# Linear attention with an MLP behind it: q of batches 1 to 7 transposed by a DMA instead of TensorE, input weights loaded in 64-partition pieces

## The chip, the cores and the metric

One core of a Trainium2 chip runs the whole kernel. The metric is device time in microseconds (us); the kernel before took 325.62 us, the median of three runs between 323.76 and 325.9.

## The reference

The shapes are batch 8, 8 heads, 576 positions, head dimension 64; the MLP goes from 512 to 2048 and back.

```python
def _attn_ref(q, k, v):
    q_s = np.exp(q - np.max(q, axis=-1, keepdims=True))
    q_s = q_s / (np.sum(q_s, axis=-1, keepdims=True) + 1e-09)
    k_s = np.exp(k - np.max(k, axis=2, keepdims=True))
    k_s = k_s / (np.sum(k_s, axis=2, keepdims=True) + 1e-09)
    kv = np.einsum('bhsd,bhse->bhde', k_s, v)
    return np.einsum('bhsd,bhde->bhse', q_s, kv)

def _moe_ref(x, w_in, w_out):
    h = x @ w_in
    g = h * (1.0 / (1.0 + np.exp(-h)))
    return g @ w_out

x = attn_out.transpose(0, 2, 1, 3).reshape(B * S, H * D)
```

The heads of a position, 8 times 64 values, stand side by side as the 512 columns of x, of which there are 8 times 576, or 4608 rows.

## The kernel before, in words

**Attention of one batch.** `load` brings q, k and v of a batch, 1152 KB each, from SP's queue into tiles of 128 partitions (two heads by 64 position groups; a partition holds 9 positions, J). `exp` takes exp on ACT to bf16 (`eq`, `ek`). `qsum` and `qnorm` normalise q: sums and reciprocals on DVE, the product on DVE or POOL. `vcast` turns v to bf16 in `vaug`, with a column of ones beside each head, so that `kv` on TensorE (PE), over 9 values of j, gives the products of k and v and the sums of k at once. `kvcopy` on DVE divides them and puts them as blocks into `kvbd`. `tr` transposes the normalised q: three groups of six 128x128 transposes on PE into PSUM (`qtps`), each copied to `qT` by `trcopy` on DVE (lines 116 to 137). `xt` multiplies `kvbd` with `qT`, the projection, once for each of four chunks of 128 columns of x, and copies the result out of PSUM to `XT`, on ACT from tile 1 on.

**The MLP.** The rows of x are cut into nine tiles: tile 0 is the 576 of batch 0 in two parts, tile 1 is 448, the others 512. `mm1` is one unit for each of 16 blocks of 128 of the 2048 columns: four matmuls for each part, then tanh on ACT and a product on DVE, into `GT`. `mm2` has 16 units a tile too, of four matmuls; after the last of a block of rows the result goes over `ost` (four buffers) to DRAM, as two stores on SP's queue. All weights are loaded once, at the start, by POOL's queue, which turns them from f32 to bf16: W_in (`W1`, in the trace `W_58`) in eight transfers of 256 KB, W_out (`W2`, `W_59`) in four.

**The order.** Batch 0 is written out first. Then a list `units` has mm1 of tile 0, mm2 of tile 0, mm1 of tile 1, mm2 of tile 1, and from there mm2 of one tile interleaved with mm1 of the next. `plan_attn` puts each step of a batch's attention ahead of a unit, counted from the first mm1 unit of the batch's tile: `sm` for the two halves of exp of q and of k, `tp` for the transposes, `ks` for kv, `ox` for the projections. Each engine executes what it was given in this order. SP's queue has no units of its own: a load or store there waits only for its data, its buffer and what stands ahead of it. Loads of batch 1 are held back by a one-element copy on POOL (line 399) that reads the last element of W_in. Projections and transposes share one PSUM buffer (tag `aps`).

## Time and profile before

| | |
|---|---|
| median of three runs | 325.62 us |
| the profiled execution | 325.91 us |
| its span, first to last instruction | 324.1 us |
| mean granted clock of TensorE in the span | 0.969 |
| TensorE busy | 293.5 us (91%) |
| DVE, ACT, POOL busy | 164.3, 162.3, 42.7 us |
| moved by DMA | 42.26 MB |

The span is shorter than the profiled execution by 1.8 us, which lie around it. Busy time of TensorE includes matmuls that overlap the next, so a stage with busy time near its length is full, not necessarily at its peak. A line of the timeline gives start, length, engine and line of code, instruction, the tile written and the tiles read, and in brackets the idle time ahead of it and what ended that. A granted clock of 1.0 is 2.4 GHz, 0.5 is 1.2 GHz.

### The profile page before, as it was taken

The page shows a single profiled execution, that of the slowest core. Times are in us where ns is not written, and L with a number is a line of the kernel's source. Part 1 is how long each engine was busy: PE and PEld are TensorE (multiplying, and loading weights), DVE is VectorE, ACT ScalarE, POOL GpSimd, SP SyncE. Part 2 cuts the span into 40 slices and gives each one's busy share as a digit, 9 for nine tenths or more (in the row PEclk, how much of TensorE's full clock was granted, in tenths as well). Part 3 has the DMA queues.
Part 4 walks back from the last instruction along what each step waited for, and adds up shares of the span by engine and source line. Part 5 has one row for each costly group of instructions (what it writes and reads, how often), then busy time and mean ns, then how long its engine had stood idle before and what let it go on. Part 6 is the DMA issues. An engine that isn't in the chain of part 4 may idle for free.

```text
span 324.1 us, 4484 instructions
## 1 busy us (share of the span) xinstructions
PE 293.5 (91%) x1723; PEld 142.5 (44%) x1723; DVE 164.3 (51%) x312; ACT 162.3 (50%) x266; POOL 42.7 (13%) x40
## 2 busy tenths in 40 slices
PE   5617998997889789899999999999999999999993
PEld 1404654553445334445444444444444444444441
DVE  4813889378927655753375348534543333343300
ACT  5603773278157467566465646654345446444220
POOL 0803000000007025250025003400000000000000
PEclk9976999999799989999999999999999999999998
DMA  7899999971857715758211111111201211111222
GB/s 285 181 165 144 263 329 397 392 244 20 307 183 230 271 40 209 260 172 258 74 32 34 32 32 34 32 33 34 47 22 46 49 34 32 32 32 35 64 66 66
DMA packets 28933, 42.26 MB, mean 130 GB/s; under 512 B 8944, under 2 KB 10992, under 8 KB 28912
## 3 DMA queue, kind: packets, MB, share of 16 engines
q1 hardware_dynamic: 18480, 37.76, 36.8%
q0 software_dynamic: 10432, 4.22, 9.3%
q8 instruction: 13, 0.21, 0.3%
q14 instruction: 8, 0.07, 0.1%
HBM read 36.70 MB, written 9.44 MB: 142 GB/s over the span
## 4 chain that ended last, share of the span: by engine, by line
PE 71%; DMA 10%; DVE 10%; ACT 4%; issue 2%; POOL 1%; SPq 0%; DVEq 0%; ACTq 0%
PE hps L195 35%; PE ops L228 28%; DMA W_58<-in_moe_w_in_dram 5%; DMA vt<-in_v_dram 4%; DVE zq L103 3%; DVE GT L211 2%; PE kvps L144 2%; PE ops L324 2%; ACT sg L203 2%; PE qtps L121 2%; DVE eq L109 2%; DMA kt<-in_k_dram 2%; ACT eq L89 1%; POOL W_58 L273 1%; DVE rzq L104 1%
## 5 line engine op out<-in xcount | busy, mean ns | idle before, releaser
L211 DVE SCALAR_TENSOR_TENSOR GT<-sg,hps 128x512 bf16<-128x512 f32 (+2 forms) x176 | 101.7, 587 | 126.2 <-ACT sg L203 123.2
L195 PE MATMUL hps<-XT,W_58 128*128 128x512 bf16 (+2 forms) x640 | 149.0, 364 | 9.0 <-DMA W_58<-in_moe_w_in_dram 8.9
L203 ACT ACTIVATE sg<-hps 128x512 f32<-128x512 f32 (+2 forms) x160 | 88.4, 554 | 110.5 <-PE hps L195 109.3
L228 PE MATMUL ops<-W_59,GT 128*128 128x512 bf16 x512 | 130.1, 383 | 0.0
L195 PEld LDWEIGHTS <-W_58 128*128 128x128 bf16 x640 | 61.8, 99 | 74.2 <-DMA W_58<-in_moe_w_in_dram 10.7
L228 PEld LDWEIGHTS <-GT 128*128 128x128 bf16 x512 | 49.0, 99 | 55.4 <-issue 2.0
L109 POOL TENSOR_TENSOR eq<-eq,rzq 128x1152 bf16<-128x1152 bf16 x10 | 21.1, 2117 | 143.2 <-PE hps L195 126.9
L243 ACT ACTIVATE ost<-ops 128x512 f32<-128x512 f32 x34 | 20.2, 597 | 21.7 <-PE ops L228 21.4
L103 DVE TENSOR_REDUCE zq<-eq 128x18 f32<-128x1152 bf16 x16 | 21.5, 1346 | 3.4 <-ACT eq L89 3.4
L121 PE MATMUL qtps<-ident,eq 128*128 128x128 bf16 x144 | 13.0, 233 | 8.0 <-DVE eq L109 5.4
L89 ACT ACTIVATE eq<-qt 128x1152 bf16<-128x1152 f32 x16 | 18.4, 1159 | 2.5 <-DMA qt<-in_q_dram 2.5
L89 ACT ACTIVATE ek<-kt 128x1152 bf16<-128x1152 f32 x16 | 18.3, 1160 | 1.1 <-DMA kt<-in_k_dram 1.1
L121 PEld LDWEIGHTS <-eq 128*128 128x128 bf16 x144 | 10.3, 104 | 15.6 <-DVE eq L109 6.8
L324 PE MATMUL ops<-W_59,GT 128*128 128x512 bf16 x64 | 15.3, 379 | 0.0
L136 DVE COPY qT<-qtps 128x768 bf16<-128x768 bf16 (+1 forms) x32 | 13.7, 447 | 2.4 <-PE qtps L121 2.3
L144 PEld LDWEIGHTS <-ek 64*128 64x128 bf16 x288 | 9.1, 98 | 10.6 <-issue 8.5
L324 PEld LDWEIGHTS <-GT 128*128 128x128 bf16 x64 | 6.1, 98 | 6.3
L109 DVE TENSOR_TENSOR eq<-eq,rzq 128x1152 bf16<-128x1152 bf16 x6 | 8.1, 1357 | 0.2
L144 PE MATMUL kvps<-vaug_61,ek 64*128 64x130 bf16 x144 | 5.9, 227 | 2.2 <-DVE kvbd_62 L158 2.2
L144 PE MATMUL kvps<-vaug_60,ek 64*128 64x130 bf16 x144 | 6.0, 228 | 1.8 <-ACT vaug_60 L94 1.4
L96 POOL CAST vaug_61<-vt 128x1152 bf16<-128x1152 f32 x6 | 6.8, 1156 | 0.0
L273 POOL DMA_DIRECT2D W_58<-in_moe_w_in_dram x8 | 6.5, 862 | 0.0
(138 smaller groups left out, 87.6 us busy)
## 6 DMA issues: line engine op xcount, KB each, us to landing
out_dram<-ost SPq DMA_DIRECT2D x72, 128.0 KB, 2.4
qt<-in_q_dram SPq DMA_DIRECT2D x7, 1152.0 KB, 6.5
kt<-in_k_dram SPq DMA_DIRECT2D x7, 1152.0 KB, 6.9
vt<-in_v_dram SPq DMA_DIRECT2D x7, 1152.0 KB, 6.3
W_58<-in_moe_w_in_dram POOLq DMA_DIRECT2D x8, 256.0 KB, 15.2
W_59<-in_moe_w_out_dram POOLq DMA_DIRECT2D x4, 512.0 KB, 16.1
qt<-in_q_dram SPq DMA_DIRECT2D x2, 576.0 KB, 4.1
kt<-in_k_dram SPq DMA_DIRECT2D x2, 576.0 KB, 7.1
```

Of the source, the lines that this page charges most:

```text
L89: nc.scalar.activation(out=o, in_=jgd(st[b][src], cc), func=ACT.Exp)
L103: nc.vector.reduce_sum(out=st[b]["zq"][:, cc], in_=e, axis=AX.X)
L109: eng.tensor_tensor(out=e, in0=e, in1=r[:, :, :, None].to_broadcast([128, J, 2, D]), op=ALU.mult)
L121: nc.tensor.transpose(out=t[:, i * 128:(i + 1) * 128], in_=st[b]["eq"][:, j, cc * 128:(cc + 1) * 128], identity=ident,)
L136: nc.vector.tensor_copy(o, t[:, :, i:i + n, :])
L144: nc.tensor.matmul(out=st[b]["kvps"][:, r, cc * 256:cc * 256 + 2 * E1], lhsT=st[b]["ek"][r * P:(r + 1) * P, j, cc * 128:(cc + 1) * 128], r ...
L195: nc.tensor.matmul(out=hps[:, 0:size], lhsT=W1[:, c, fb * 128:(fb + 1) * 128], rhs=XT[t][:, c, off:off + size], start=(c == 0), stop=(c == ...
L203: nc.scalar.activation(out=sg[:, 0:size], in_=hps[:, 0:size], func=ACT.Tanh, scale=0.5)
L211: nc.vector.scalar_tensor_tensor(out=GT[g][:, fb, col:col + n], in0=sg[:, h], scalar=1.0, in1=hps[:, h], op0=ALU.add, op1=ALU.mult,)
L228: nc.tensor.matmul(out=OP[t, tb], lhsT=GT[t][:, fc, tb * 128:(tb + 1) * 128], rhs=W2[:, fc, :], start=(fc == 0), stop=(fc == NFB - 1),)
L243: nc.scalar.activation(out=ost, in_=OP[t, tb], func=ACT.Copy, scale=0.5)
L324: nc.tensor.matmul(out=OP[t, tb], lhsT=GT[t][:, fc, tb * 128:(tb + 1) * 128], rhs=W2[:, fc, :], start=(fc == 0), stop=(fc == NFB - 1),)
```

## The change

The transposes of q of batches 1 to 7 leave TensorE: `tr_dma` issues one transposing DMA on SP's queue for a batch, from `eq` to `qT` in SBUF, 576 KB, in 18 blocks of 128x128; batch 0 keeps `tr` and `trcopy`. `qT` is now laid out in j blocks, so `xt` reads columns in pieces of 64. Tile 0 is cut at 320 instead of 288 columns, a multiple of 64. W_in comes in 16 transfers of 64 partitions and a quarter of the columns (the four of one quarter first), instead of eight of 128 partitions and half of the columns. Loads of batch b + 2 are planned right behind the transpose of batch b. The plans move: batch 2 is prepared from 21 units ahead instead of 11, with POOL instead of DVE for `qnorm` and `vcast`; batches 3 and 4 by a few units; the projections of batch 2 by two.

```diff
--- before.py
+++ after.py
@@ -40,7 +40,7 @@
     NCH = NT // TCH
 
     cut = [0, S] + [TCH * (t + 2) for t in range(NCH - 1)]
-    part = [[(0, S // 2), (S // 2, S // 2)]] + [[(0, cut[t + 1] - cut[t])] for t in range(1, NCH)]
+    part = [[(0, 5 * P), (5 * P, S - 5 * P)]] + [[(0, cut[t + 1] - cut[t])] for t in range(1, NCH)]
     E1 = D + 1
     assert J * P == S and D == 64 and NG == 4 and DM == H * D and NT == NCH * TCH
 
@@ -111,29 +111,34 @@
         )
 
 
+    def qt_tile(b):
+        if "qT" not in st[b]:
+            st[b]["qT"] = ap.tile([128, J, 2, 128], BF16, name="qT")
+        return st[b]["qT"]
+
+    def tr_dma(b, eng):
+        eng.dma_start_transpose(
+            out=qt_tile(b).rearrange("x j c y -> x (j c) y"),
+            in_=st[b]["eq"].rearrange("x j y -> x (j y)"),
+        )
+
     TG = 6
 
-    def tr(b, g, tag="aps"):
-        t = ps.tile([128, TG * 128], BF16, name="qtps", tag=tag, bufs=PSB[tag])
+    def tr(b, g):
+        t = ps.tile([128, TG, 128], BF16, name="qtps", tag="hps", bufs=PSB["hps"])
         st[b]["qtps", g] = t
         for i in range(TG):
             cc, j = divmod(g * TG + i, J)
             nc.tensor.transpose(
-                out=t[:, i * 128:(i + 1) * 128],
-                in_=st[b]["eq"][:, j, cc * 128:(cc + 1) * 128],
-                identity=ident,
+                out=t[:, i, :], in_=st[b]["eq"][:, j, cc * 128:(cc + 1) * 128], identity=ident
             )
 
     def trcopy(b, g):
-        if "qT" not in st[b]:
-            st[b]["qT"] = ap.tile([128, 2, 2, J * P], BF16, name="qT")
-        t = st[b]["qtps", g].rearrange("x (j r p) -> x r j p", r=2, p=P)
         i = 0
         while i < TG:
             cc, j = divmod(g * TG + i, J)
             n = min(J - j, TG - i)
-            o = st[b]["qT"][:, cc, :, j * P:(j + n) * P].rearrange("x r (j p) -> x r j p", p=P)
-            nc.vector.tensor_copy(o, t[:, :, i:i + n, :])
+            nc.vector.tensor_copy(qt_tile(b)[:, j:j + n, cc, :], st[b]["qtps", g][:, i:i + n, :])
             i += n
 
     def kv(b, cc):
@@ -177,7 +182,7 @@
                 nc.tensor.matmul(
                     out=o1[:, a - first:a - first + n],
                     lhsT=kvbd[b % 3][:, c, :],
-                    rhs=st[b]["qT"][:, cc, r, col:col + n],
+                    rhs=st[b]["qT"][:, col // P:(col + n) // P, cc, r * P:(r + 1) * P],
                 )
                 a += n
             x = XT[t][:, c, off:off + size]
@@ -266,15 +271,15 @@
 
 
     nc.gpsimd.tensor_copy(gate[:, 0:1], st[0]["vt"][0:1, 1, 0:1])
-    FH = DFF // 2
-    w_in_v = w_in.rearrange("(c g r d) f -> c r g d f", g=2, r=2, d=D)
-    for i in range(2):
-        for c in range(NC):
-            nc.gpsimd.dma_start(
-                out=W1[:, c, i * FH:(i + 1) * FH],
-                in_=w_in_v[c // 2, c % 2][:, :, i * FH:(i + 1) * FH],
-            )
     FQ = DFF // 4
+    w_in_v = w_in.rearrange("(c g r d) f -> g d c r f", g=2, r=2, d=D)
+    for i in range(4):
+        for g in range(2):
+            for cc in range(2):
+                nc.gpsimd.dma_start(
+                    out=W1[g * 64:(g + 1) * 64, 2 * cc:2 * cc + 2, i * FQ:(i + 1) * FQ],
+                    in_=w_in_v[g][:, cc, :, i * FQ:(i + 1) * FQ],
+                )
     for i in range(4):
         nc.gpsimd.dma_start(
             out=W2[:, i * 4:(i + 1) * 4, :],
@@ -296,13 +301,13 @@
     vcast(0, 0, nc.scalar)
     exp(0, "kt", "ek", 1)
     vcast(0, 1, nc.scalar)
-    tr(0, 0, "hps")
+    tr(0, 0)
     trcopy(0, 0)
     kv(0, 0)
     kvcopy(0, 0)
     heat(1)
     for g in (1, 2):
-        tr(0, g, "hps")
+        tr(0, g)
         trcopy(0, g)
     kv(0, 1)
     kvcopy(0, 1)
@@ -372,22 +377,17 @@
 
 
 
-        if b + 2 < B:
-            lag = 6 if eng[1] is nc.gpsimd else 1
-            for i, (name, src) in enumerate((("qt", q), ("kt", k), ("vt", v))):
-                plan(
-                    u + sm[3 if i else 1] + 1 + lag * (i > 1),
-                    lambda name=name, src=src: load(b + 2, name, src),
-                )
         for cc in range(2):
             plan(u + sm[cc], lambda cc=cc: exp(b, "qt", "eq", cc))
             plan(u + sm[cc] + 1, lambda cc=cc: (qsum(b, cc), qnorm(b, cc, eng[cc])))
         for cc in range(2):
             plan(u + sm[2 + cc], lambda cc=cc: exp(b, "kt", "ek", cc))
             plan(u + sm[2 + cc], lambda cc=cc: vcast(b, cc, eng[cc]))
-        for g in range(3):
-            plan(u + tp[g], lambda g=g: tr(b, g))
-            plan(u + tp[g] + 1, lambda g=g: trcopy(b, g))
+        plan(u + tp, lambda: tr_dma(b, nc.sync))
+        if b == 1:
+            plan(u + tp, lambda: [load(2, n, x) for n, x in (("kt", k), ("vt", v))])
+        if b + 2 < B:
+            plan(u + tp + 1, lambda: [load(b + 2, *x) for x in (("qt", q), ("kt", k), ("vt", v))])
         for cc in range(2):
             plan(u + ks[cc], lambda cc=cc: kv(b, cc))
             plan(u + ks[cc] + 1, lambda cc=cc: kvcopy(b, cc))
@@ -399,14 +399,14 @@
     nc.gpsimd.tensor_copy(st[1]["qt"][64:65, 0, 0:1], W1[64:65, 3, DFF - 1:DFF])
     for name, src in (("qt", q), ("kt", k), ("vt", v)):
         load(1, name, src)
-    plan(14, lambda: [load(2, n, x) for n, x in (("qt", q), ("kt", k), ("vt", v))])
+    plan(14, lambda: load(2, "qt", q))
     V = nc.vector
-    plan_attn(1, begin[1], (-14, -12, -10, -9), (-8, -7, -6), (-5, -4), (-4, -3, -2, -1), (V, V))
-    plan_attn(2, begin[2], (-11, -10, -9, -8), (-7, -4, -3), (-5, -2), (-2, -1, -1, 0), (V, V))
-    plan_attn(3, begin[3], (-23, -21, -19, -17), (-14, -12, -10), (-8, -7), (-5, -4, -3, -2))
-    plan_attn(4, begin[4], (-40, -37, -34, -31), (-22, -19, -16), (-13, -11), (-9, -7, -5, -3))
+    plan_attn(1, begin[1], (-14, -12, -10, -9), -6, (-5, -4), (-4, -3, -2, -1), (V, V))
+    plan_attn(2, begin[2], (-21, -17, -13, -9), -9, (-7, -5), (-4, -3, -2, -1))
+    plan_attn(3, begin[3], (-26, -24, -22, -20), -13, (-9, -7), (-6, -5, -4, -3))
+    plan_attn(4, begin[4], (-42, -38, -34, -30), -20, (-12, -10), (-9, -7, -5, -3))
     for b in range(5, B):
-        plan_attn(b, begin[b], (-56, -52, -48, -44), (-26, -22, -18), (-13, -11), (-9, -7, -5, -3))
+        plan_attn(b, begin[b], (-56, -52, -48, -44), -22, (-13, -11), (-9, -7, -5, -3))
     for c in range(NC):
         plan(begin[NCH - 1] - 9 + 2 * c, lambda c=c: xt(NCH - 1, c))
```

On SP's queue, before, behind the loads of batch 0. The three loads of each batch follow each other (the numbers tell the buffers apart: qt_243 is batch 1, qt_490 batch 2, qt_562 batch 3), then come the stores of tile 0.

```order
L78 DMA qt_243<-in_q_dram 128x4x576
L78 DMA kt_246<-in_k_dram 128x4x576
L78 DMA vt_248<-in_v_dram 128x4x576
L78 DMA qt_490<-in_q_dram 128x4x576
L78 DMA kt_492<-in_k_dram 128x4x576
L78 DMA vt_494<-in_v_dram 128x4x576
L78 DMA qt_562<-in_q_dram 128x4x576
L78 DMA kt_584<-in_k_dram 128x4x576
L78 DMA vt_597<-in_v_dram 128x4x576
L247 DMA out_0_dram<-ost_701 64x512 x2
```

After, the same place: qt_251 is batch 1, qt_498 batch 2, qt_604 batch 3.

```order
L78 DMA qt_251<-in_q_dram 128x4x576
L78 DMA kt_254<-in_k_dram 128x4x576
L78 DMA vt_256<-in_v_dram 128x4x576
L78 DMA qt_498<-in_q_dram 128x4x576
L120 DMA_TRANSPOSE qT_594<-eq_546 128x18x128
L78 DMA kt_596<-in_k_dram 128x4x576
L78 DMA vt_598<-in_v_dram 128x4x576
L78 DMA qt_604<-in_q_dram 128x4x576
L78 DMA kt_606<-in_k_dram 128x4x576
L78 DMA vt_608<-in_v_dram 128x4x576
L252 DMA out_0_dram<-ost_685 64x512 x2
```

The transpose of batch 1 stands between q and k of batch 2, so it is issued ahead of five loads and behind four.

On DVE, before, from the mm1 units of tile 1 (GT with 448 columns) to the first kv block of batch 2 (kvbd_64):

```order
L211 SCALAR_TENSOR_TENSOR GT<-sg,hps 128x448 x15
L103 TENSOR_REDUCE zq<-eq 128x18
L104 RECIPROCAL rzq<-zq 128x18
L109 TENSOR_TENSOR eq<-eq,rzq 128x9x128
L211 SCALAR_TENSOR_TENSOR GT<-sg,hps 128x448
L103 TENSOR_REDUCE zq<-eq 128x18
L104 RECIPROCAL rzq<-zq 128x18
L109 TENSOR_TENSOR eq<-eq,rzq 128x9x128
L96 CAST vaug_60<-vt 128x9x2x64 x2
L136 COPY qT<-qtps 128x2x384
L155 RECIPROCAL rz<-kvps 128x4
L158 TENSOR_TENSOR kvbd_64<-kvps,rz 64x2x64 x2
```

After, the same stretch, from the end of tile 0:

```order
L246 TENSOR_SCALAR ost<-ops 128x512 x2
L216 SCALAR_TENSOR_TENSOR GT<-sg,hps 128x448 x5
L103 TENSOR_REDUCE zq<-eq 128x18
L104 RECIPROCAL rzq<-zq 128x18
L216 SCALAR_TENSOR_TENSOR GT<-sg,hps 128x448 x4
L103 TENSOR_REDUCE zq<-eq 128x18
L104 RECIPROCAL rzq<-zq 128x18
L216 SCALAR_TENSOR_TENSOR GT<-sg,hps 128x448 x7
L160 RECIPROCAL rz<-kvps 128x4
L163 TENSOR_TENSOR kvbd_64<-kvps,rz 64x2x64 x2
L160 RECIPROCAL rz<-kvps 128x4
L163 TENSOR_TENSOR kvbd_64<-kvps,rz 64x2x64 x2
```

The sums of batch 2 now stand among the products of mm1 of tile 1 instead of behind the fifteenth; its normalising product, its casts of v and the copies of qT are gone from DVE.

## Rows read from the trace of the kernel before

**Rows 1.** The page's part 2: TensorE's busy tenths in 40 slices of 8.1 us.
```profile
PE   5617998997889789899999999999999999999993
```

**Rows 2.** Stages: PE, PEld, DVE, ACT, POOL busy us (instructions), granted clock, DMA share, GB/s.
```profile
17.30:27.40 10.10, 1.27 (x3) 0.31 (x3) 0.00 (x0) 0.40 (x1) 2.31 (x3) 0.66 1.12 163
...
34.00:46.00 12.00, 11.98 (x85) 7.37 (x85) 10.16 (x32) 8.62 (x22) 0.00 (x0) 1.00 1.13 297
...
46.70:65.10 18.40, 17.00 (x122) 8.35 (x121) 11.53 (x22) 6.84 (x10) 0.00 (x0) 1.00 1.05 390
...
77.50:95.00 17.50, 13.67 (x102) 6.55 (x100) 11.45 (x20) 7.41 (x12) 0.00 (x0) 0.90 0.70 233
95.00:124.00 29.00, 25.86 (x157) 12.22 (x155) 18.25 (x33) 19.09 (x30) 10.69 (x7) 0.94 0.53 182
```

**Rows 3.** Timeline of PE around the first matmul of W_in: start us, us, instruction, idle before.
```profile
16.98 0.28 PE L177 MATMUL o_240<-qT,kvbd_62 128*128 128x288 bf16 x1 [0.36 <-ACT XT L187]
23.30 0.42 PE L195 MATMUL hps<-XT,W_58 128*128 128x288 bf16 x1 [6.03 <-DMA W_58<-in_moe_w_in_dram]
...
27.41 19.27 PE L195 MATMUL hps<-XT,W_58 128*128 128x288 bf16 x125 [1.25 <-DMA W_58<-in_moe_w_in_dram]
```

**Rows 4.** Timeline of POOL (weight issues, gate) and of SP's queue (batches 1, 2).
```profile
9.52 6.54 POOL L273 DMA_DIRECT2D W_58<-in_moe_w_in_dram  x8
...
30.57 0.18 POOL L399 CAST qt<-W_58 1x1 f32<-1x1 bf16 x1 [2.18 <-DMA W_58<-in_moe_w_in_dram]
...
31.98 0.58 SPq L78 DMA_DIRECT2D vt<-in_v_dram  x1
32.68 5.76 SPq L78 DMA_DIRECT2D qt<-in_q_dram  x1
```

**Rows 5.** DMA view: first W_in issue (KB, us to landing); packets, MB, share in 18:22.
```profile
W_58<-in_moe_w_in_dram POOLq DMA_DIRECT2D x1, 256.0 KB, 13.7
...
q0 software_dynamic: 351, 0.72, 101.4%
```

**Rows 6.** DMA view, queues: W_out alone in 30:33, loads alone in 50:56.
```profile
q0 software_dynamic: 470, 0.47, 111.8%
...
q1 hardware_dynamic: 1067, 2.38, 104.0%
```

**Rows 7.** DMA view: landings of v of batch 1 and q of batch 2.
```profile
vt<-in_v_dram SPq DMA_DIRECT2D x1, 1152.0 KB, 19.6
...
qt<-in_q_dram SPq DMA_DIRECT2D x1, 1152.0 KB, 21.9
```

**Rows 8.** The page's part 6: stores, and loads of 576 KB (median us to landing).
```profile
out_dram<-ost SPq DMA_DIRECT2D x72, 128.0 KB, 2.4
...
qt<-in_q_dram SPq DMA_DIRECT2D x2, 576.0 KB, 4.1
```

**Rows 9.** Timeline of PE: a group of six transposes between units of mm2.
```profile
87.58 0.50 PE L121 MATMUL qtps<-ident,eq 128*128 128x128 bf16 x6
87.92 1.03 PE L228 MATMUL ops<-W_59,GT 128*128 128x512 bf16 x4
88.79 0.51 PE L121 MATMUL qtps<-ident,eq 128*128 128x128 bf16 x6
```

**Rows 10.** Waits of PE: us in total, times, longest us.
```profile
PE qtps L121 <- DVE eq L109: 5.4, 2, 3.0
PE qtps L121 <- DVE qT L136: 2.3, 2, 1.4
PE kvps L144 <- DVE kvbd_62 L158: 2.2, 1, 2.2
```

**Rows 11.** Timeline of DVE: first and last normalising instruction of batch 1.
```profile
48.22 1.35 DVE L103 TENSOR_REDUCE zq<-eq 128x18 f32<-128x1152 bf16 x1 [0.53 <-ACT eq L89]
...
52.86 1.36 DVE L109 TENSOR_TENSOR eq<-eq,rzq 128x1152 bf16<-128x1152 bf16 x1
```

**Rows 12.** Timeline of PE: the first projection matmul of batch 1.
```profile
60.91 0.36 PE L177 MATMUL o_672<-qT,kvbd_63 128*128 128x448 bf16 x1
```

## Prediction

> **What bounds the kernel now.** I read the page's slices first: the reader is to see TensorE (PE) weak in slices 0 to 3 (0 to 32 us), patchy up to about 130 us, and at nine tenths in every slice from the twentieth on [rows 1]. So the second half is bound by TensorE's own instructions, and only the first 130 us hold waits.
>
> The stage table sizes them [rows 2]. From 17.3 to 27.4 us PE is busy 1.27 of 10.1 us. The timeline says why: the last projection matmul of batch 0 starts at 16.98, the first matmul of W_in stands still until 23.30, and the stream runs only from 27.41, each start released by a landing of W_in [rows 3]. The granted clock is at its lower level (0.5, 1.2 GHz) for part of that stage (mean 0.66), after PE had idled. From 77.5 to 95 us PE is busy 13.67 of 17.5 us, 3.8 us idle; the clock's mean of 0.90 says that a fifth of the stage, 3.5 us, ran at half speed, another 1.75 us lost: 5.6 us in all. From 95 to 124 the same reading gives 3.1 idle plus 1.75, 4.9 us. From 46.7 to 65.1 it is 1.4 us idle. The waits of PE name the releasers: DVE for the normalised q (5.4 us, of which 2.5 in batch 2), DVE for the copies of transposed q out of PSUM (2.3 us: 1.4 in batch 1, 0.9 in batch 4), and DVE for a kv block (2.2 us) [rows 10].
>
> **The start: W_in in 64-partition transfers.** Before, POOL issues eight transfers in 6.54 us, 0.82 each [rows 4], and the first lands 13.7 us after its issue, for 256 KB [rows 5]. That is not bandwidth: from 18 to 22 us the software queue moved only 351 packets while its packets took 101% of 16 engines' time, so 4 us × 16 / 351 = 0.185 us for a packet of 2 KB; 128 of them over sixteen engines would need 1.5 us, over two engines 11.8 us. The measured 13.7 fits two engines, with eight transfers side by side; so all of the first four, which the first unit needs, come late and together.
> The new transfers have 64 partitions on either side and 128 pieces of 1 KB each, the pieces of W_out's transfers. For those the trace has a rate: 470 packets in 3 us, 157 per us [rows 6], 0.82 us for a transfer if all engines share it. Issue and data then run at the same pace. The fourth is issued by 9.52 + 4 × 0.82 = 12.8 and landed 2.4 us later (the landing time of a small store [rows 8]), at 15.2. The activations XT of batch 0 are ready at about 17.5, so XT, and not W_in, starts the first unit: 17.5 instead of 27.4, and with hardly any idle time ahead of it I expect no half clock there. The price from both sides: at best this 9.9 us, at worst nothing, if the new transfers stay on few engines.
> The Trainium skill has a rule for either end. DMA: Bandwidth & Descriptors, Rules for kernel authors, says of two transfers to disjoint partition halves not to bother, because both spread over all sixteen engines and use the same ones: by that the start stays at 27.4 and this edit only adds eight issues. The same page, Why a DMA increments its semaphore by 16 and not by 1, says that the number of engines is the largest up to 16 that divides the slowest dimension of both sides: 2 and 128 before (two engines), 64 and 64 after (sixteen). The 351 packets agree with the second rule.
>
> **What is late next.** The first matmul layer of tile 0 runs at 85 matmuls in 12 us at the full clock [rows 2], so its 128 take 18.1 us: 17.5 to 35.6. Then mm2 of tile 0, 0.87 us a unit [rows 9], would reach its eleventh unit at 45.2, where kv of batch 1 stands. That work needs loads, and they have moved by less: they start when the last W_in transfer has landed, at 30.57 before [rows 4]; now sixteen plus four issues at 0.82 end at 25.9, so about 26.0, 4.6 us earlier. The issues and landings of before [rows 4, 7] shifted by 4.6: v of batch 1 (issued 31.98, landed 19.6 us later) 51.6 to 47.0, q of batch 2 (32.68 + 21.9) 54.6 to 50.0. q of batch 1 stands two loads of 2.97 us (1152 KB at 2.38 MB in 6 us [rows 6]) ahead of v, so at about 41.1; one us of exp and DVE's 6.0 us of normalising (48.22 to 54.22 [rows 11]) end at 48, inside this. kv of batch 1 starts at 47.0 plus a cast of 0.8, a wait of 2.6 us.
>
> **The crossbar transpose.** Removed: 126 transposes of batches 1 to 7 on TensorE, 21 groups of six at 0.34 us (87.58 to 87.92 [rows 9]), and 28 copies on DVE, which cost nothing where DVE isn't late. Added: seven transposing DMAs of 576 KB on SP's queue. The trace shows none. From below: 576 KB at 2.38 MB per 6 us [rows 6] is 1.5 us. From above: 256 KB took 13.7 us where the shape was bad [rows 5], so a shape can cost ten times the bytes' time. The nearest row has the same 576 KB through the same queue: 4.1 us [rows 8]. I take 4.1, and keep 1.5 and 13.7 for the range.
> The skill's page has a rate for it (same page, Latency and other measured facts: 261 GB/s), by which it would be 2.3 us plus a fixed 2, an estimate of 4.3; no run here shows it yet.
> In batch 1 the transpose stands on SP behind q of batch 2, as the order excerpt shows, so it begins at 50.0 and lands at 54.1, and the projection (60.91 before [rows 12]) waits for it: 6.8 us earlier than before. SP holds behind it k and v of batch 2 and all of batch 3: five loads of 2.97 us, landed at 69.0; k and v of batch 2, the first two, are read after 65 us and q of batch 3 after 76, so I cost that at nothing. The two waits on PE (2.6 us for v, then up to 4 for qT) may pull the clock down as the idle time at 17.3 did; most of the slower stretch lies under the wait for qT, and I charge 1.0 us.
> In batch 2 the transpose waits on SP for the loads of batch 3 to land (a store ahead of it takes their completion counter): issued about 69, landed 73; the projection is due at 59.3 + 16 × 0.87 × 7/8 + 1.0 + 4 × 0.87 = 76. Batches 3, 4 and 5 to 7 have 7, 11 and 13 units between transpose and projection, 6.1, 9.6 and 11.3 us. So 4.1 us is hidden everywhere but in batch 1; the cover ends at about 7, 6, 10 and 11 us. The stores behind a transpose on SP are held for no longer than it; four output buffers, each filled over four units of 0.87 us or more, hide that. The cut of tile 0 at 320 columns leaves 128 matmuls and the same columns, at no cost.
>
> **Batches 2 and 3 prepared earlier.** The exps of batch 2 move from 11 to 21 units ahead, into mm1 of tile 1, and its normalising from DVE to POOL. The 5.6 us lost between 77.5 and 95 go; DVE and ACT now do this work beside the mm1 units, and I charge 1.0 us (between 0 and the 5.6 it costs today). Of the 4.9 us between 95 and 124 the waits for PSUM copies and back-to-back kv sets are eased, the exps of batch 4 in ACT's order stay: I take half, 2.5.
>
> **The sum**, on the profiled execution (325.91 us, span 324.1, 1.8 around it): projection of batch 1 −6.8 + 1.0 = −5.8 (the three transpose groups of batch 1, its 1.4 us wait and the start are inside this); batch 2 −5.6 + 1.0 = −4.6; 95 to 124 −2.5; the qT wait of batch 4 −0.9; eighteen transpose groups of batches 2 to 7 × 0.34 = −6.1. Together −19.9: span 304.2, time 306.0. The median of the runs shown is 325.62, 0.3 below the profiled one, which changes nothing.
>
> **Rivals.**
> W_in no faster: the transfers go on landing near 27 us. For it: twice as many POOL issues, of which the later wait for landings of earlier ones; against it: the 351 packets. Then the loads keep their places, qT of batch 1 comes at 54.6 + 4.1 = 58.7, 2.2 before 60.91 instead of 5.8: 309.6 us.
> Projections slower: qT now lies in blocks of 64 columns, and no row shows a matmul that reads its moving side so. At half speed 18,432 columns more, at 0.87 us for 2,048, are 7.8 us: 313.8. Nothing in the trace speaks for it.
> A middling transpose, 8 us: batch 1 +3.9, batch 2 +0.9, batch 3 +1.9: 312.7.
> Slower: the crossbar takes the time of a badly shaped transfer, in place of bytes' time. Beyond its cover each batch stalls PE for the rest: at 11 us 6.9 + 3.9 + 4.9 + 1.4 = 17.1, at 12 us 23.2, so from about 11.5 us the kernel loses. At 13.7 us it is 9.6 + 6.6 + 7.6 + 4.1 + 3 × 2.4 = 35.1: 341 us. For it: W_in in this very trace; against it: a load of the same bytes through the same queue takes 4.1 [rows 8].
>
> **How the numbers follow.** Forecast 0.62, W_in no faster 0.13, slower projections 0.08, middling transpose 0.08, all four faster; slower 0.09. A measurement of this kernel tells about 1% (3 us) from no change; for "same" a transpose close to 11 us has to meet a late W_in, and I take 0.06 out of the middle cases: faster 0.85, same 0.06, slower 0.09. The forecast's own range: a transpose of 1.5 us (−2.6), no half clock (−1.0), no cost of the moved work (−1.0) and all of 95 to 124 gained (−2.4) give 299, and stalls of the later stages that I left alone some 3 us more, 296. Upwards it takes in the late W_in, the middling transpose and the slow projections, to 317.
>
> **What would show it.** Right: first W_in matmul near 17.5 without a wait on W_in, granted clock 1.0 from 17 to 40 us, loads of batch 1 issued near 26, the projection of batch 1 at 54 with the transpose as its releaser, no PE wait on DVE for qT, transposes landing in about 4 us. Wrong: PE waits on W_in after 20 us, a projection waiting for qT in batches 3 to 7, or projection matmuls longer than before.

## The result, and the profile after

The changed kernel takes 307.17 us (median of 4 runs, 305.58 to 307.5), the kernel before 325.76 beside it (323.76 to 326.09): a ratio of 0.9432, with a 95% interval of 0.9382 to 0.9482. The forecast was 306.0. Put on a chip once more, beside the last experiments, the changed kernel took 305.78 (305.47 to 307.76), ratio 0.9388 (0.9341 to 0.9436). Its profiled execution took 307.5 us, with a span of 305.7. Two experiments (W_in alone, every transpose twice) had one execution longer than their others, the profiled one: it is left out of their times, and of those two traces only one wait each, a DMA's landing and packet counts are read.

TensorE's slices of the changed kernel, and the clock granted to it, to be held against [rows 1]:

```profile
PE   5679995878999799989999999999999999999993
...
PEclk9579999999999999999999999999999999999999
```

A slice is now 7.6 us. Slice 2 (15 to 23 us) stands at 7 where before slices 2 and 3 stood at 1 and 7; 5, 8, 7, 8 (46 to 76 us) is the new weak place, a 7 stands at 99 to 107 us, and from 138 us on all but the last are at nine tenths. The stages, with the columns of [rows 2]:

```profile
17.30:27.40 10.10, 8.82 (x53) 5.36 (x53) 5.84 (x19) 5.49 (x14) 5.95 (x9) 0.83 1.07 158
...
58.50:74.00 15.50, 12.82 (x66) 6.29 (x65) 12.21 (x21) 11.86 (x20) 5.57 (x4) 1.00 0.95 350
74.00:91.50 17.50, 17.23 (x114) 8.17 (x113) 8.19 (x16) 12.11 (x17) 7.18 (x5) 1.00 0.84 266
91.50:120.00 28.50, 26.08 (x154) 12.10 (x152) 16.60 (x29) 18.62 (x30) 6.53 (x5) 1.00 0.57 174
```

PE is busy 8.82 of the 10.1 us in which it was busy 1.27. The mm2 stage of tile 1 (74 to 91.5) is full, where the same stage of before lost 5.6 us; but mm1 of tile 1 (58.5 to 74) has 2.7 us idle in it.

To see where the time went I took the start of the first activation sg<-hps of each tile from ACT's timeline, in us of the span. It follows the tile's first mm1 unit.

| | before | changed | predicted gain, this stretch | measured gain, this stretch |
|---|---|---|---|---|
| tile 1 | 66.09 | 59.48 | 5.8 | 6.6 |
| tile 2 | 96.17 | 85.53 | 5.6 | 4.0 |
| tile 3 | 124.20 | 110.68 | 3.5 | 2.9 |
| tile 4 | 156.25 | 141.96 | 1.9 | 0.8 |
| tile 8 | 278.21 | 260.29 | 3.1 | 3.6 |
| end of span | 324.13 | 305.73 | 0 | 0.5 |

The predicted column divides the sum by stretches, with 1.0 us for each batch's three transpose groups (the 2.5 us of "95 to 124" stand with tile 3). Together 19.9 predicted, 18.4 measured. This mark can stand late, behind an exp on ACT, and before it did so in tile 2. By TensorE's first mm1 matmul of the tile (65.14, 94.43 and 155.19 before; 58.53, 84.47 and 140.90 changed) tile 2 gained 3.4 us, where 5.6 were predicted, and tiles 3 and 4 together 4.3, where 5.4 were.

The timeline of PE in the changed kernel, at the start, in batch 1 and in mm1 of tile 1:

```profile
17.68 0.43 PE L200 MATMUL hps<-XT,W_58 128*128 128x320 bf16 x2
19.12 1.81 PE L200 MATMUL hps<-XT,W_58 128*128 128x320 bf16 x7 [1.01 <-DMA W_58<-in_moe_w_in_dram]
...
50.23 0.69 PE L149 MATMUL kvps<-vaug_61,ek 64*128 64x130 bf16 x18 [2.34 <-DVE vaug_61 L96]
...
54.32 0.35 PE L182 MATMUL o_656<-qT,kvbd_63 128*128 128x448 bf16 x1 [1.82 <-DMA qT<-eq]
...
64.64 0.92 PE L200 MATMUL hps<-XT,W_58 128*128 128x448 bf16 x4 [0.50 <-DVE GT L216]
66.68 3.19 PE L200 MATMUL hps<-XT,W_58 128*128 128x448 bf16 x16 [1.12 <-DVE GT L216]
70.93 3.19 PE L200 MATMUL hps<-XT,W_58 128*128 128x448 bf16 x16 [1.06 <-DVE GT L216]
```

The first W_in matmul stands at 17.68 (23.30 before [rows 3]), with one wait of 1.01 us behind it, where before 6.03 us stood ahead of it and 1.25 behind. The projection of batch 1 is released by the transposing DMA at 54.32 (60.91 before [rows 12]). The three waits on GT are new.

POOL's timeline, SP's timeline and the DMA view say what stands behind those waits:

```profile
9.80 6.73 POOL L279 DMA_DIRECT2D W_58<-in_moe_w_in_dram  x11
19.27 0.59 POOL L279 DMA_DIRECT2D W_58<-in_moe_w_in_dram  x1 [2.73 <-DMA W_58<-in_moe_w_in_dram]
...
27.83 0.18 POOL L399 CAST qt<-W_58 1x1 f32<-1x1 bf16 x1 [2.05 <-DMA W_58<-in_moe_w_in_dram]
```

```profile
29.12 0.71 SPq L78 DMA_DIRECT2D vt<-in_v_dram  x1
29.95 5.41 SPq L78 DMA_DIRECT2D qt<-in_q_dram  x1
45.84 6.39 SPq L120 DMA_TRANSPOSE qT<-eq  x1
...
72.68 2.73 SPq L120 DMA_TRANSPOSE qT<-eq  x1
```

The landings, from the DMA view in the stretch of each issue (first W_in transfer; v of batch 1; q of batch 2; transpose of batch 1), and for all seven transposes:

```profile
W_58<-in_moe_w_in_dram POOLq DMA_DIRECT2D x1, 128.0 KB, 3.7
...
vt<-in_v_dram SPq DMA_DIRECT2D x1, 1152.0 KB, 20.1
...
qt<-in_q_dram SPq DMA_DIRECT2D x1, 1152.0 KB, 22.3
...
qT<-eq SPq DMA_TRANSPOSE x1, 8.4
...
qT<-eq SPq DMA_TRANSPOSE x7, 4.7
```

The first W_in transfer lands after 3.7 us, where [rows 5] had 13.7; over all of them the median is 6.5 on the page of the changed kernel and 15.2 on that of before. POOL's eleven first issues go out at once; the twelfth waits 2.73 us for a landing, a later one 0.33, and the last transfer lands at 27.8 and opens the gate for the loads of batch 1 (30.57 before [rows 4]). v of batch 1 then lands at 49.2, q of batch 2 at 52.25, the transpose of batch 1 at 54.24.

### The profile page after: what moved, and what is told of

Read it like the earlier page. It is cut to its first block, busy times and chain, and to the rows that moved or that the text cites. A ratio compares the mean times of both kernels' runs of the same rounds, so it can differ in the third digit from the quotient of the medians.

```text
span 305.7 us, 4237 instructions
## 1 busy us (share of the span) xinstructions
PE 281.9 (92%) x1597; PEld 135.2 (44%) x1597; DVE 148.9 (49%) x280; ACT 162.5 (53%) x266; POOL 52.3 (17%) x52
## 3 DMA queue, kind: packets, MB, share of 16 engines
q0 software_dynamic: 4416, 4.20, 9.3%
## 4 chain that ended last, share of the span: by engine, by line
PE 74%; DMA 15%; DVE 4%; ACT 2%; POOL 2%; issue 1%; SPq 1%; ACTq 0%; DVEq 0%; POOLq 0%
PE ops L233 35%; PE hps L200 34%; DMA vt<-in_v_dram 8%; DMA W_58<-in_moe_w_in_dram 4%; DMA qT<-eq 3%; PE kvps L149 2%; POOL W_58 L279 1%; DVE GT L216 1%; DVE zq L103 1%; PE ops L329 1%; ACT sg L208 1%; ACT eq L89 1%; SPq L80 0%; DVE kvbd_62 L163 0%; ACT XT L192 0%
## 5 line engine op out<-in xcount | busy, mean ns | idle before, releaser
L216 DVE SCALAR_TENSOR_TENSOR GT<-sg,hps 128x512 bf16<-128x512 f32 (+2 forms) x176 | 100.4, 586 | 114.4 <-ACT sg L208 113.5
L200 PE MATMUL hps<-XT,W_58 128*128 128x512 bf16 (+3 forms) x640 | 147.0, 361 | 3.7 <-DVE GT L216 2.7
L208 ACT ACTIVATE sg<-hps 128x512 f32<-128x512 f32 (+3 forms) x160 | 88.3, 554 | 96.4 <-PE hps L200 94.9
L233 PE MATMUL ops<-W_59,GT 128*128 128x512 bf16 x512 | 128.6, 379 | 0.0
L109 POOL TENSOR_TENSOR eq<-eq,rzq 128x1152 bf16<-128x1152 bf16 x12 | 25.4, 2117 | 123.0 <-ACT eq L89 56.8
L89 ACT ACTIVATE ek<-kt 128x1152 bf16<-128x1152 f32 x16 | 18.4, 1156 | 5.7 <-DMA kt<-in_k_dram 5.7
L89 ACT ACTIVATE eq<-qt 128x1152 bf16<-128x1152 f32 x16 | 18.4, 1159 | 2.4 <-DMA qt<-in_q_dram 2.4
L329 PE MATMUL ops<-W_59,GT 128*128 128x512 bf16 x64 | 14.9, 379 | 0.0
L279 POOL DMA_DIRECT2D W_58<-in_moe_w_in_dram x16 | 9.7, 642 | 3.2 <-DMA W_58<-in_moe_w_in_dram 3.1
L96 POOL CAST vaug_61<-vt 128x1152 bf16<-128x1152 f32 x6 | 6.8, 1157 | 0.0
L96 POOL CAST vaug_60<-vt 128x1152 bf16<-128x1152 f32 x6 | 6.8, 1155 | 0.0
L293 PE MATMUL wps<-warm 128*128 128x512 bf16 x11 | 4.8, 599 | 1.2 <-DVE warm L258 1.2
L109 DVE TENSOR_TENSOR eq<-eq,rzq 128x1152 bf16<-128x1152 bf16 x4 | 5.4, 1357 | 0.1
L132 PE MATMUL qtps<-ident,eq 128*128 128x128 bf16 x18 | 2.3, 313 | 3.3 <-DVE eq L109 3.3
```

The source lines that it names most:

```text
L89: nc.scalar.activation(out=o, in_=jgd(st[b][src], cc), func=ACT.Exp)
L96: eng.tensor_copy(o, jgd(st[b]["vt"], cc))
L109: eng.tensor_tensor(out=e, in0=e, in1=r[:, :, :, None].to_broadcast([128, J, 2, D]), op=ALU.mult)
L200: nc.tensor.matmul(out=hps[:, 0:size], lhsT=W1[:, c, fb * 128:(fb + 1) * 128], rhs=XT[t][:, c, off:off + size], start=(c == 0), stop=(c == ...
L208: nc.scalar.activation(out=sg[:, 0:size], in_=hps[:, 0:size], func=ACT.Tanh, scale=0.5)
L216: nc.vector.scalar_tensor_tensor(out=GT[g][:, fb, col:col + n], in0=sg[:, h], scalar=1.0, in1=hps[:, h], op0=ALU.add, op1=ALU.mult,)
```

## The experiments

Twelve experiments. Where a ratio is given, it is to the kernel before on the same chip (325.93, 326.07 and 326.08 us in the three sets); the first tile starts are those of each kernel's profiled execution. "Changed" is the kernel of the change, 307.17 us, and 305.78 in the third set.

**1 and 2: the two halves of the change.** Experiment 1 puts the new W_in loop alone into the kernel before; experiment 2 puts the old one back into the changed kernel.

```diff
 (2)
-    w_in_v = w_in.rearrange("(c g r d) f -> g d c r f", g=2, r=2, d=D)
+    FH = DFF // 2
+    w_in_v = w_in.rearrange("(c g r d) f -> c r g d f", g=2, r=2, d=D)
...
+                out=W1[:, c, i * FH:(i + 1) * FH],
```

> The kernel before with the new W_in transfers alone. My theory: the whole start is W_in's and the gain reaches the second tile, because nothing on PE waits for a transposing DMA here. First W_in matmul at 17.7, mm1 of tile 0 done at 38, batch 1's casts of v at 49 as in the changed kernel, first mm1 of tile 1 at 55 to 56 instead of 65.1, the later stalls of before unchanged: 316 us (314 to 318). Rival: the loads of later batches then come too late and eat it: 320 or more, with waits on q, k or v in batch 2 or 3.

> The changed kernel with the old W_in transfers. My theory: the transpose of batch 1 stands behind q of batch 2, which lands at about 54.6 as before, so the projection of batch 1 starts at 57 to 58 instead of 54.3 and all that follows moves by 3 to 4: 310.5 us (309 to 312). Rival, the two parts simply add: 9 to 10 us are lost, 316 to 317. Rival, W_in was hidden anyway: 307.

W_in alone: 319.24 (318.67 to 321.3), ratio 0.9794 (0.9722 to 0.9866), less than the expected gain. All but W_in: 312.48, ratio 0.9576 (0.9512 to 0.964), 5.3 us above the changed kernel; its tile 1 starts at 64.42 instead of 59.48, and its gate opens at 30.82. The two ratios give 6.7 and 13.8 us, together 20.5, against 18.5 for both at once; with some 2 us of uncertainty on each this can't be told from a plain sum: that one half needs the other doesn't show. In the trace of experiment 1 the largest new wait is PE for a copy of qT in batch 1 (5.8 us): the transposes of batch 1 had become what is late. That led to the next one.

**3 and 9: transposes of batches 1 to 7 back on TensorE, the rest as changed.** Experiment 3 places the three groups of a batch one to three units apart; experiment 9 spreads them in batches 2 to 7.

```diff
-        plan(u + tp, lambda: tr_dma(b, nc.sync))
+        for g, p in enumerate(TP[min(b, 5)]):
+            plan(u + p, lambda g=g: tr(b, g))
+            plan(u + p + 1, lambda g=g: trcopy(b, g))
...
 (9, in TP)
-        2: (-9, -8, -7),
-        3: (-13, -12, -11),
...
+        2: (-9, -7, -5),
+        3: (-14, -12, -10),
...
```

In both the groups use the projections' PSUM buffer again, as before.

> The changed kernel with q of batches 1 to 7 transposed on PE again (at the unit where the DMA was issued and the next ones), with the W_in transfers, the plans and the places of the loads kept. My theory: 18 groups of 0.34 us in batches 2 to 7 come back, 6.1 us, and a us of waits for the one PSUM buffer; batch 1 wins the 1.8 us wait for the DMA and pays 1.0 for its groups: 313 us (311 to 315). Rival, the moved plans and not the crossbar made the gain: 307 to 309. Rival, DVE's copies cost as well: above 316.

> As the run with all transposes on PE, but with the three groups of a batch as far apart as before the change (four and three units instead of one to three). My theory: the crossbar's gain has two parts, PE's own 0.34 us a group and PE's waits for the copy of qT out of the one PSUM buffer, which DVE does in its order; the second depends on the distance. In batches 2 to 7 the waits (6 us in that run) fall to 2 or less and only the 6 us of the groups stay, batch 1 keeps its 5.3 us behind the casts of v: 317 to 319 us. Rival, the distance is not it and something else costs with PE transposes: 321 to 323 as before.

Experiment 3: 322.64, ratio 0.9877 (0.9807 to 0.9947), ten us above what was expected. Experiment 9: 316.71, ratio 0.9719 (0.9662 to 0.9777). PE's waits in 3, then in 9:

```profile
PE qtps L132 <- DVE qT L141: 11.7, 7, 5.3
```

```profile
PE qtps L132 <- DVE qT L141: 5.4, 2, 4.5
```

So some 6 us of experiment 3 were groups that stood too close: the next group waits until DVE has copied the last one out of PSUM. Of the wait that is left, 4.5 us stand in batch 1. DVE's timeline there, and PE's, in experiment 9:

```profile
46.97 1.55 DVE L96 CAST vaug<-vt 128x1152 bf16<-128x1152 f32 x2 [3.03 <-DMA vt<-in_v_dram]
48.44 0.54 DVE L141 COPY qT<-qtps 128x768 bf16<-128x768 bf16 x1
```

```profile
49.03 0.80 PE L132 MATMUL qtps<-ident,eq 128*128 128x128 bf16 x6 [4.50 <-DVE qT L141]
```

The copy of qT doesn't wait for its own data: it is queued on DVE behind the casts of v, and these wait for v's load. With transposes on TensorE, a load that the transposes don't need stops TensorE. The transposing DMA does away with that; TensorE then waits for v at kv itself, later in its program, 2.3 us in one execution of the changed kernel and not at all in the other (experiment 12). On one chip, PE transposes spread out cost 316.71 − 305.78 = 10.9 us: 3.5 at the start of tile 1 (61.02 against 57.54) and 7.6 from there to tile 8 (208.43 against 200.81). The first part is no pure price of the transposes: the granted clock of experiment 9 was at its lower level from 46.6 to 53.4 us, that of experiment 12 at full there, and against the other execution of the changed kernel (59.48) it is 1.5.

**4: W_in in sixteen transfers of the old shape.** Half the bytes per transfer, but 128 partitions, and a source that is cut 2 by 64 as before.

```diff
+    w_in_v = w_in.rearrange("(c g r d) f -> c r g d f", g=2, r=2, d=D)
...
+                out=W1[:, c, i * FQ:(i + 1) * FQ],
+                in_=w_in_v[c // 2, c % 2][:, :, i * FQ:(i + 1) * FQ],
```

> The changed kernel with W_in in sixteen transfers of 128 partitions and a quarter of the columns, so as small and as many as the new ones (128 KB), but with the old shape of the source (two by 64 rows). Theory of the engines: each stays on two engines, 64 packets of about 0.105 us each, 6.7 us, so the first lands 7 to 9 us after its issue instead of 3.7 and the first unit starts near 20; 308 to 310 us. Rival, the size alone: it lands in 3.7 us and starts at 17.7, 307. Rival, 128 partitions are slow whatever the size: 13 us to landing, start near 25.

One run: 315.09, where 308 to 310 was expected; the landing came as expected. The first landing, and POOL's gate:

```profile
W<-in_moe_w_in_dram POOLq DMA_DIRECT2D x1, 128.0 KB, 8.0
```

```profile
36.01 0.18 POOL L398 CAST qt<-W 1x1 f32<-1x1 bf16 x1 [1.26 <-DMA W<-in_moe_w_in_dram]
```

128 KB in this shape take 8.0 us, in the new one 3.7. The smaller size alone takes the landing from 13.7 to 8.0, but the kernel is then no faster than with the old transfers (312.48): what made it fast is the shape. 256 KB took 13.7 [rows 5]: the second 128 KB cost 5.7 us. W_in is read as f32, twice the bytes that are written, so that is 46 GB/s, where all sixteen engines move 2.38 MB in 6 us [rows 6], or 25 GB/s for each: by this estimate a transfer on about two engines. The software queue in the microsecond from 13 to 14 us, with four or five transfers issued before, and five to seven of half the size changed:

```profile
q0 software_dynamic: 712, 0.05, 70.5%
```

```profile
q0 software_dynamic: 181, 0.17, 110.3%
```

More than three times the bytes move in the new shape. And TensorE starts early here too (17.94), but the gate opens 8.2 us later than in the changed kernel and tile 1 starts 7.6 later (67.05): what batch 1 waits for is the last landing of W_in, not the first. The page's software queue of before, of the changed kernel and of experiment 4:

```profile
q0 software_dynamic: 10432, 4.22, 9.3%
```

```profile
q0 software_dynamic: 4416, 4.20, 9.3%
```

```profile
q0 software_dynamic: 18752, 4.25, 12.0%
```

The same bytes, but 14,336 packets more in experiment 4 than in the changed kernel: 896 small ones for each of its sixteen transfers. Before there were as many for each of the eight: 18752 − 10432 is 8 × 1040, so a transfer of the old shape is 1040 packets at either size, and one of the new shape 144. Few engines and small packets come together in every run, and no run separates them; but from 18 to 22 us before, the 351 packets of 0.72 MB [rows 5] leave no room for small ones, and the transfers landed late all the same.

**5: every transposing DMA twice.** The first of the two writes a tile that nobody reads; it is work added, the output is the same.

```diff
+        eng.dma_start_transpose(
+            out=again.rearrange("x j c y -> x (j c) y"),
+            in_=st[b]["eq"].rearrange("x j y -> x (j y)"),
+        )
```

> The changed kernel with each transposing DMA issued twice, the first into a tile that nobody reads. My theory: a transpose holds SP's queue for 2.8 us and lands in 4.7, and outside batch 1 there is room for a second. Batch 1's projection starts 2.8 to 4.7 later than 54.3, batch 2's about 0.5 later still, the others not: 310 to 312.5 us. Rival, the cover of the later batches is thin: 2.8 us more in each of seven, 325 or more. Rival, everything is hidden: 307.

312.35 (311.33 to 312.7), ratio 0.957 (0.9524 to 0.9617): some 5 us more than the changed kernel for seven transposes more. The added one lands after 4.9 us (median of 7). TensorE's only wait for qT:

```profile
PE o L188 <- DMA qT<-eq: 2.9, 1, 2.9
```

That fits the price of one batch, batch 1, with a second transpose hidden in the other six as well. The mean granted clock of that trace, 0.84, makes the units longer and the cover wider, so the time is the better evidence.

**6, 10 and 11: what the transpose of batch 1 waits for.** Experiment 6 issues q of batch 2 behind that transpose instead of ahead of it. Experiment 10 adds to this the sums (and products) of q of batch 2 two units later, experiment 11 a gate on the third quarter of W_in instead of the last.

```diff
 (6)
-            plan(u + tp, lambda: [load(2, n, x) for n, x in (("kt", k), ("vt", v))])
+            plan(u + tp, lambda: [load(2, n, x) for n, x in (("qt", q), ("kt", k), ("vt", v))])
...
-    plan(14, lambda: load(2, "qt", q))
 (10, besides)
-            plan(u + sm[cc] + 1, lambda cc=cc: (qsum(b, cc), qnorm(b, cc, eng[cc])))
+            plan(u + sm[cc] + (3 if b == 2 else 1), lambda cc=cc: (qsum(b, cc), qnorm(b, cc, eng[cc])))
 (11, besides)
-    nc.gpsimd.tensor_copy(st[1]["qt"][64:65, 0, 0:1], W1[64:65, 3, DFF - 1:DFF])
+    nc.gpsimd.tensor_copy(st[1]["qt"][64:65, 0, 0:1], W1[64:65, 3, 3 * FQ - 1:3 * FQ])
```

> The changed kernel with q of batch 2 loaded behind the transpose of batch 1 instead of ahead of it. My theory: the transpose is issued at 45.8 as now, but only v of batch 1 (landed at 49.2) is ahead of it, so it lands by 52 instead of 54.2; the projection then waits for the kv blocks alone (52.4), 1.8 us earlier, and q of batch 2 comes about 57, ahead of its exp at 62: 305.4 us. Rival, the late q of batch 2 gives the gain back: 307, or a wait of ACT on q of batch 2.

> The version with the transpose of batch 1 ahead of q of batch 2, and in batch 2 the sums of q two units further behind their exps. My theory: PE waits on DVE's product in mm1 of tile 1 because ACT's exp delays a tanh by 1.2 us and DVE's sum, one unit on, delays the product by another 1.3, more than three PSUM buffers cover; apart, each is covered. Of the 2.7 us of waits 1.5 to 2.5 go: 303 us. Rival, the two engines simply have too much to do in those units: 305.

> The version with the transpose of batch 1 ahead of q of batch 2, and batch 1's loads held back to the third quarter of W_in. With the transpose out of the way, v of batch 1 is late next; it lands 1.3 us earlier. My theory: PE then waits for v a little as now, tile 1 starts at 54 to 55.5 instead of 55.95: 304 us (303 to 305). Rival, the wait for v stays and the half clock that follows it takes the gain: 305 to 306.5.

Experiment 6: 305.11 (304.32 to 306.66), ratio 0.9364 (0.9325 to 0.9403). SP's timeline and PE's:

```profile
46.71 2.84 SPq L120 DMA_TRANSPOSE qT<-eq  x1
```

```profile
49.52 0.69 PE L149 MATMUL kvps<-vaug,ek 64*128 64x130 bf16 x18 [0.81 <-DVE vaug L96]
...
51.73 0.36 PE L182 MATMUL o<-qT,kvbd 128*128 128x448 bf16 x1
```

The transpose holds SP for 2.84 us instead of 6.39, lands in 4.7 instead of 8.4, and no projection waits for it. The gain in time, by the ratios, is not clear of noise. Experiment 10: 303.91 (303.16 to 305.01), ratio 0.9315 (0.9266 to 0.9364); its six runs all lie below the six of the changed kernel beside it (305.47 to 307.76). It is the best version found, but not for the reason expected. TensorE's waits on GT, of which 1.5 to 2.5 of 2.7 us were to go:

```profile
PE hps L200 <- DVE GT L216: 2.2, 3, 1.1
```

Only 0.5 us went, and in the profiled executions (experiment 10's was the slowest of its six) tile 1 starts as in experiment 12, 57.44 against 57.54. Where the rest of the gain comes from stays open. Experiment 11: 305.39 (303.84 to 306.44), ratio 0.936 (0.9313 to 0.9407): the earlier gate gives nothing more.

**7: the exps of q of batch 2 six and eight units earlier.**

```diff
-    plan_attn(2, begin[2], (-21, -17, -13, -9), -9, (-7, -5), (-4, -3, -2, -1))
+    plan_attn(2, begin[2], (-27, -25, -13, -9), -9, (-7, -5), (-4, -3, -2, -1))
```

> The changed kernel with the exps, sums and products of q of batch 2 planned at units 29 and 31, into the end of mm2 of tile 0, instead of units 35 and 39 inside mm1 of tile 1. My theory: the 3.1 us that mm1 of tile 1 lost come from them (PE waits on DVE's product, three times 0.5 to 1.1 us); DVE is idle there for 4.9 us and ACT for most of a unit. Two of three go, and the casts of the projections on ACT stand behind the exps for about 0.6 us each: 305 to 306 us, waits of PE on GT gone or halved. Rival, the casts of the projections wait a whole exp each and PE with them: 307 or more.

306.41, ratio 0.9398 (0.9363 to 0.9433): undecided as a change. PE's waits on GT, in experiment 7 and in the changed kernel:

```profile
PE hps L200 <- DVE GT L216: 1.4, 2, 0.9
```

```profile
PE hps L200 <- DVE GT L216: 2.7, 3, 1.1
```

Half of them went, but the stretch did not get shorter. PE's timeline in experiment 7:

```profile
60.23 0.92 PE L200 MATMUL hps<-XT,W 128*128 128x448 bf16 x4 [0.42 <-ACT ost L248]
61.83 1.67 PE L200 MATMUL hps<-XT,W 128*128 128x448 bf16 x8 [0.69 <-DVE ost L246]
64.41 8.48 PE L200 MATMUL hps<-XT,W 128*128 128x448 bf16 x44 [0.91 <-DVE GT L216]
73.39 0.92 PE L200 MATMUL hps<-XT,W 128*128 128x448 bf16 x4 [0.50 <-DVE GT L216]
```

The moved exps and sums now stand among the copies of the last results of tile 0, and the second and third unit of mm1 wait for these instead. From its first matmul to the first of mm2, mm1 of tile 1 takes 15.3 us (58.89 to 74.15), in the changed kernel 15.4. The eleven units in one piece, where the changed kernel stopped three times, show that the waits move with the exps and sums. (The first activation, the mark of the table, comes at 61.10 here, late behind an exp; by that mark the stretch would seem 1.4 us shorter.) Ahead of tile 1 the granted clock was at its lower level from 50.0 to 56.8 us.

**8: the gate on the third quarter of W_in,** alone (the edit of experiment 11).

> The changed kernel with the loads of batch 1 held back until the third quarter of W_in has landed instead of the last. My theory: the last landing of W_in (27.8) is late next; the loads start at about 26.0, when POOL has issued the weights, and q, k, v of batch 1, q of batch 2 and the transpose behind it come 1.5 to 1.9 us earlier: 305.5 us. Rival, the DMA engines are full from 24 to 54 us, the loads only share earlier and the landings move by half of that or less: 306.5 to 307; the last quarter of W_in would then be late for mm1 of tile 0.

307.8 (305.62 to 308.96), ratio 0.9431 (0.9393 to 0.947): nothing. The loads of batch 1 start at 25.0, 3.0 us earlier, yet v lands only 1.3 earlier (47.9); the loads now run beside the last of W_in and W_out, which I take for the reason. And TensorE, idle 2.9 us for v, then ran at the lower clock from 48.2 to 55.0.

**12: the changed kernel again,** beside experiments 9 to 11.

> The changed kernel once more, beside these: 307 us (305.5 to 308), for the comparison on one chip. The granted clock falls after idle stretches of PE between 5 and 55 us, at other places than in the first trace, and moves the first matmul of tile 1 by up to 2 us.

305.78, as given above. In this execution v took 18.8 us to land instead of 20.1, and PE's timeline has no wait for it:

```profile
48.61 0.68 PE L149 MATMUL kvps<-vaug,ek 64*128 64x130 bf16 x18
...
52.37 0.35 PE L182 MATMUL o<-qT,kvbd 128*128 128x448 bf16 x1 [1.49 <-DMA qT<-eq]
```

Tile 1 starts at 57.54 instead of 59.48; from there to the end both executions take 246.3 us. Between these two executions the whole difference lies ahead of tile 1, in the arrival of v of batch 1 and of q of batch 2 (50.3 instead of 52.25).

## Why the prediction was right

**The start** was right in kind: XT, not W_in, starts mm1 of tile 0 (17.68, predicted 17.5). The reading of the 351 packets, two engines to a transfer, fits what experiment 4 measured; the engines themselves no view shows. The Trainium skill, DMA: Bandwidth & Descriptors, Rules for kernel authors, would have had the split into partition halves change nothing; here it took the landing from 13.7 to 3.7 us, and experiment 4 shows that the halving of the bytes gives only 8.0. The same page's count of engines (Why a DMA increments its semaphore by 16 and not by 1) is the rule that the measurement follows. What was mis-sized is "landed 2.4 us later" for the fourth transfer, which the first unit also needs: the third and fourth took 5.8 us in the median, TensorE stood 1.01 us until 19.12, and the clock was at its lower level from 18.6 to 22.0, so tile 0's mm1 ended at about 38.3 instead of 35.6. It cost nothing, because v is later: in experiment 11 mm1 of tile 0 ended 3.4 us earlier than in experiment 12 and tile 1 started 0.5 earlier.

**What is late next** was named rightly and priced 2 us too early: the gate at 27.83 instead of 25.9, v at 49.2 (47.0), q of batch 2 at 52.25 (50.0). The step "sixteen plus four issues at 0.82 end at 25.9" was the right time for the issues (25.78), by luck: an issue took 0.61 us and not 0.82, but POOL's twelfth stood still for 2.73 us and a later one for 0.33. What it left out is that the gate waits for a landing, 2.05 us more.

**The transpose** takes 4.7 us, where I took 4.1 and kept 1.5 to 13.7. By the Trainium skill's rate (same page, Latency and other measured facts) my estimate was 4.3, 0.4 short. In batch 1 two errors met: q of batch 2 landed 2.2 us later, but the transpose needed only 2.0 us after it, where a transpose alone takes 4.7; SP had held its issue from 45.84 to 52.23, until that landing. So the projection of batch 1 came at 54.32, predicted 54.1, by luck. The 1.0 us for a slower clock there was not paid, and the gain is 6.6 instead of 5.8. In batches 2 to 7 no projection waits for a transpose, and the time of experiment 5 fits that there was room for a second one.

**The eighteen groups of batches 2 to 7** were priced at 6.1 us plus 0.9 for a wait on qT, 7.0; experiment 9 against 12 gives 7.6 from tile 1 to tile 8.

**Batch 2** is the step that was mis-sized: "DVE and ACT now do this work beside the mm1 units, and I charge 1.0 us". It costs 3.2: from its first matmul to the first of mm2, mm1 of tile 1 takes 15.4 us (58.53 to 73.95) instead of 12.2 (65.14 to 77.39 before), 2.7 of it waits on GT. These 2.2 us beyond the charge are what tile 2 fell short of. DVE's timeline in the changed kernel:

```profile
64.50 1.34 DVE L103 TENSOR_REDUCE zq<-eq 128x18 f32<-128x1152 bf16 x1
...
68.75 1.35 DVE L103 TENSOR_REDUCE zq<-eq 128x18 f32<-128x1152 bf16 x1
```

Two of the three waits, 2.2 us, end with a product that stood behind one of these sums; the products free PSUM for TensorE. The first, 0.5 us, ends with a product whose tanh stood on ACT behind an exp of 1.16 us. This is read from the timelines; experiment 7 shows that the waits move with this work, and experiment 10 that two more units between exp and sum save only 0.5. No run with the new plan made mm1 of tile 1 as short as before.

**Batch 4** gave 0.8 instead of 1.9: the wait on qT is gone, but another took its place. PE's timeline of before, and of the changed kernel:

```profile
135.79 0.49 PE L121 MATMUL qtps<-ident,eq 128*128 128x128 bf16 x6 [0.94 <-DVE qT L136]
```

```profile
130.76 0.69 PE L149 MATMUL kvps<-vaug_60,ek 64*128 64x130 bf16 x18 [1.27 <-DVE kvbd_63 L163]
```

DVE's timeline there, changed:

```profile
129.30 0.69 DVE L216 SCALAR_TENSOR_TENSOR GT<-sg,hps 128x512 bf16<-128x512 f32 x1 [1.76 <-ACT sg L208]
129.91 0.17 DVE L160 RECIPROCAL rz<-kvps 128x4 f32<-128x4 f32 x1
```

The two sets of kv are as far apart as before (2.5 us), but the plan moved them by one unit, so that an mm1 unit and not an mm2 unit follows the first set. DVE copies that set out behind the unit's product, which waits for ACT's tanh. This was read from the timeline, and no run moved it.

**The rivals.** W_in no faster is experiment 2: 312.5 where the rival said 309.6; 0.5 of the 2.9 us is tile 1 (64.42, by the rival 63.9), the rest batches 2 and 4 as above. Slower projections: 0.35 us for 448 columns, as before [rows 12]. A slow transpose: 4.7 us at every batch but the first, far from the 11.5 at which the kernel would have lost. What stays open is when the lower clock comes: waits of TensorE of 2.4 and 1.2 us at 46 to 54 us went with it in experiment 7, one of 2.9 in experiment 8, but 2.3 and 1.8 not in the changed kernel. Open, too, are the 0.5 us gained behind the start of tile 8.

## What to carry to other kernels

When a transfer lands far later than its bytes explain, look at its shape and its packets before its size: the same bytes in another cut can land in less than half the time (128 KB in 3.7 us instead of 8.0). A transpose moved from TensorE to a DMA saves more than its matmuls, because the copies out of PSUM leave a queue in which they waited for other work; but it should stand on its DMA queue ahead of loads that are not yet needed (here 1.8 us of waiting). And when a first stall goes, price the gate behind it by the last landing, not by the last issue.

## What the hardware did that was not expected

- A transfer of W_in in the old shape carries 896 small packets of 4 bytes more than one in the new shape (18752 − 4416 = 16 × 896), whatever its size; both have 128 of data. What they are for, the trace doesn't say.
- Seven transposing DMAs more (experiment 5) are 16,352 packets more on the hardware queue and 4.13 MB: 2,336 for each, of some 250 bytes. In this form 576 KB land in 4.7 us, against 4.1 for a plain load of as many bytes [rows 8], and SP is held 2.8 us for the issue, or 6.4 where loads are still queued ahead of it.
